# Down projection: h's high half times both halves of w2 in one product of 256 columns, the second sums evicted by ScalarE and added by GpSimd

## The chip, the cores and the metric

The kernel runs on one core of a Trainium2 chip (trn2). The metric is the device time of one execution in microseconds (us), median of several runs. The engines are PE (TensorE), DVE (VectorE), ACT (ScalarE), POOL (GpSimd) and SP (SyncE, which here only issues transfers).

## The reference

Attention with pooled keys comes first, and its rows go through a mixture of 8 experts, of which each row uses the one with the largest gate logit. The change lies wholly in the second part:

```python
def _moe_ref(x, w_skip, w_gate, w1, w2):          # x: 49152 rows of 128, F = 1024
    do_compute = x @ w_skip > 0
    xc = x[do_compute]
    logits = xc @ w_gate
    e_idx = np.argmax(logits, axis=1)
    ...                                           # gate_w: softmax weight of the chosen expert
    for e in range(8):
        mask = e_idx == e
        h = np.maximum(xc[mask] @ w1[e], 0.0)
        y[mask] = gate_w[mask, None] * (h @ w2[e])
    out = x.copy()
    out[do_compute] = xc + y
```

## The kernel before

The attention part writes its rows to a scratch buffer sorted by expert. The expert part takes them in **steps** of 512 rows (`ST`), four steps (`NST`) to a group of 2048 rows of one expert. There are 72 steps: 24 "peeled" ones (`peel`, written out, interleaved with the end of the attention), then a loop (`For_i`) whose body is one group, four stages s = 0 to 3, run for 12 iterations.

float32 numbers are split into two float16 halves, a high and a low one, so each product of the mathematics is three on PE: high·high, high·low, low·high. A step consists of:

- `up(s, cs)`: for each of 8 chunks of 128 hidden columns, three products of 512 columns into a PSUM tile `h_ps` (L296 to L298; in the peeled steps it is named `up_ps`; four buffers). ACT evicts relu as `h["hi"]` (L299), then DVE makes `h["lo"]` (L300) from the same PSUM tile, and only that frees the buffer.
- `x_transpose`: ACT (L282) and DVE (L285) split rows of a later step, and SP transposes them.
- `down(s)`: 24 terms (weight half, h half, chunk), four products of 128 columns each (one for each 128 rows), accumulated in four PSUM banks `ys[t]`, traced as `acc_ps` (L311). The halves of h are the loaded weights, `w2_hi` or `w2_lo` is streamed. `w2_lo` for chunk k comes two chunks after `w2_hi` (`WL = 2`).
- `finish(s)`, called in the next step: DVE computes `o = ys[t] * gate + x` (L323) for the four t, and POOL scatters the four blocks of rows to the output (L192).

Each engine executes its instructions in program order. In the loop's stage 0 a new expert's w2 has to be split: `split_w2()` stands between `up(s, range(1, 4))` and `gates(s)`, so on ACT w2's high half (L275) follows the fourth `h_hi`, and on DVE the low half (L276) follows the fourth `h_lo`. In stage 1 DVE finds the largest weights of the next expert (`w_scale`, L209 to L217) after its part of `x_transpose`, and the next step's `o` stands behind it. In stage 2 one small product (L220) belongs to the same work.

## Time and profile before

| | us |
|---|---|
| median of 3 runs | 1737.91 (1737.71 to 1739.04) |
| the profiled execution | 1737.34 |
| its span in the trace | 1735.6 |
| of it, PE busy / DVE / ACT / POOL | 1703.6 / 1525.8 / 1265.2 / 1024.7 |

The profiled execution is one run, 1.74 us longer than the span between its first and last instruction. Busy time of PE counts pipelined products until their modelled end, so it says that PE had work, not that it streamed at its peak. Starts in the timeline are exact to 0.01 us.

### The profile page before, as it was taken

How to read it: one execution, taken by the hardware profiler on the slowest of the kernel's cores; microseconds unless marked ns; L12 is line 12 of the kernel's file. 1: busy time of each engine (PE TensorE's matmuls, PEld its weight loads, DVE VectorE, ACT ScalarE, POOL GpSimd, SP SyncE). 2: the span in 40 equal slices, each digit the busy share in tenths (PEclk: the TensorE clock that was granted, in tenths of full speed). 3: DMA queues.
4: the chain of work that ended last, by engine and by line, in shares of the span. 5: the costliest groups of instructions: out<-in, count | busy, mean ns of one | idle time of the engine just before them, and what ended most of it. 6: DMA issues, size and time to landing. Idle time of an engine off the chain costs nothing.

```text
span 1735.6 us, 51351 instructions
## 1 busy us (share of the span) xinstructions
PE 1703.6 (98%) x18801; PEld 1426.6 (82%) x18801; DVE 1525.8 (88%) x3217; ACT 1265.2 (73%) x2399; POOL 1024.7 (59%) x1292
## 2 busy tenths in 40 slices
PE   6999999999999999999999999999999999999998
PEld 5999999999999989999999777777777777777776
DVE  7989999999999999999999877777888888888887
ACT  4888888888898888888888655555555556666664
POOL 3268878888788888765668445543333333343433
PEclk9999999999999999999999999999999999999999
DMA  8999999999899999999998666222433333333333
GB/s 239 220 242 204 198 199 228 228 200 184 175 194 206 226 218 202 183 199 198 203 202 186 175 193 149 89 83 75 93 102 103 99 97 99 100 107 101 97 99 86
DMA packets 616917, 281.18 MB, mean 162 GB/s; under 512 B 502944, under 2 KB 567072, under 8 KB 616736
## 3 DMA queue, kind: packets, MB, share of 16 engines
q1 hardware_dynamic: 590192, 231.68, 64.5%
q0 software_dynamic: 21504, 38.43, 7.0%
q10 hardware_dynamic: 5040, 8.72, 1.3%
q8 instruction: 106, 1.74, 0.5%
q14 instruction: 75, 0.61, 0.1%
HBM read 85.36 MB, written 79.72 MB: 95 GB/s over the span
## 4 chain that ended last, share of the span: by engine, by line
PE 82%; DVE 11%; DMA 2%; issue 2%; POOL 1%; ACT 1%; SPq 0%; POOLq 0%; DVEq 0%; ACTq 0%
PE acc_ps L311 22%; PE acc_ps L720 17%; PE s_ps L655 6%; PE s_ps L657 6%; PE s_ps L656 5%; PE h_ps L296 5%; PE h_ps L298 5%; PE h_ps L297 5%; DVE nm L663 4%; PE acc_ps L695 4%; PE up_ps L296 2%; PE up_ps L298 2%; PE up_ps L297 2%; DVE p L677 2%; DVE ptq L703 1%
## 5 line engine op out<-in xcount | busy, mean ns | idle before, releaser
L192 POOL DMA_INDIRECT scr<-rows,di x384 | 422.2, 1099 | 170.0 <-DVE nm L663 91.5
L669 ACT ACTIVATE p_sb<-s_ps,nm 128x768 f32<-128x768 f32 x384 | 346.8, 903 | 103.9 <-DVE nm L663 100.9
L192 POOL DMA_INDIRECT out_dram<-o,xin x196 | 201.6, 1029 | 318.5 <-DVE o L323 266.0
L663 DVE TENSOR_REDUCE nm<-s_ps 128x1 f32<-128x768 f32 x384 | 365.2, 951 | 19.0 <-PE s_ps L657 17.4
L299 ACT ACTIVATE h_hi<-h_ps 128x512 f16<-128x512 f32 x384 | 223.9, 598 | 206.9 <-PE h_ps L298 193.3
L720 PEld LDWEIGHTS <-pt 128*128 128x128 f16 x4608 | 274.8, 97 | 64.7 <-issue 63.0
L720 PE MATMUL acc_ps<-v_hi,pt 128*128 128x138 f16 x3072 | 320.1, 224 | 2.7 <-DVE rs L728 1.8
L311 PEld LDWEIGHTS <-h_hi 128*128 128x128 f16 x4608 | 287.6, 98 | 15.6
L655 PE MATMUL s_ps<-k_hi,q_hi 128*128 128x384 f32 x768 | 293.4, 382 | 0.4 <-ACT k_hi L520 0.4
L720 PE MATMUL acc_ps<-v_lo,pt 128*128 128x138 f16 x1536 | 293.0, 223 | 0.0
L677 DVE SCALAR_TENSOR_TENSOR p<-p_sb,p 128x512 f16<-128x512 f32 x384 | 276.9, 721 | 5.6 <-ACT p L673 4.8
L300 DVE SCALAR_TENSOR_TENSOR h_lo<-h_ps,h_hi 128x512 f16<-128x512 f32 x384 | 245.7, 687 | 19.4 <-ACT h_hi L299 17.9
L657 PE MATMUL s_ps<-k_hi,q_lo 128*128 128x384 f32 x768 | 259.4, 338 | 0.0
L656 PE MATMUL s_ps<-k_lo,q_hi 128*128 128x384 f32 x768 | 258.1, 336 | 1.0 <-DVE k_lo L521 1.0
L673 ACT ACTIVATE p<-p_sb 128x512 f16<-128x512 f32 x384 | 242.4, 631 | 12.5 <-DMA pt<-p 9.6
L311 PE MATMUL acc_ps<-w_hi,h_lo 128*128 128x128 f16 x2304 | 222.6, 219 | 0.0
L311 PE MATMUL acc_ps<-w_lo,h_hi 128*128 128x128 f16 x2304 | 210.9, 219 | 0.0
L311 PE MATMUL acc_ps<-w_hi,h_hi 128*128 128x128 f16 x2304 | 210.9, 219 | 0.0
L299 ACT ACTIVATE h_hi<-up_ps 128x512 f16<-128x512 f32 x192 | 114.5, 597 | 109.5 <-PE up_ps L298 100.9
L720 PE MATMUL acc_ps<-v_hi,ptq 128*128 128x138 f16 x1536 | 178.0, 223 | 0.0
L323 DVE SCALAR_TENSOR_TENSOR o<-acc_ps,g_sc,xin 128x128 f32<-128x128 f32 x288 | 81.0, 344 | 104.5 <-PE acc_ps L311 100.8
L720 PE MATMUL acc_ps<-v_lo,ptq 128*128 128x138 f16 x768 | 154.9, 223 | 0.0
(200 smaller groups left out, 3393.7 us busy)
## 6 DMA issues: line engine op xcount, KB each, us to landing
q_sb<-in_q_dram SPq DMA_DIRECT2D x96, 256.0 KB
out_dram<-rows SPq DMA_DIRECT2D x96, 256.0 KB
xin<-scr SPq DMA_DIRECT2D x75, 264.0 KB, 2.9
kvt<-in_kv_dram SPq DMA_DIRECT2D x74, 256.0 KB
w_raw<-in_moe_w_dram SPq DMA_DIRECT2D x26, 512.0 KB, 3.9
scr<-pad ACTq DMA_DIRECT2D x32, 264.0 KB
pt<-p SPq DMA_TRANSPOSE x384
scr<-rows,di POOLq DMA_INDIRECT x384
```

What stands on the lines that cost most here:

```text
L192: ins = nc.gpsimd.indirect_dma_start(out=dst, out_offset=bass.IndirectOffsetOnAxis(ap=ids, axis=0), in_=src, in_offset=None, bounds_check= ...
L299: nc.scalar.activation(out=h["hi"][:, c, :], in_=ps, func=AF.Relu)
L300: paced["by"] = nc.vector.scalar_tensor_tensor(out=h["lo"][:, c, :], in0=ps, scalar=0.0, in1=h["hi"][:, c, :], op0=ALU.max, op1=ALU.subtra ...
L311: m = nc.tensor.matmul(ys[t], h[x][:, k, t * P:(t + 1) * P], w[:, k, :], start=(i == 0), stop=(i == len(terms) - 1))
L655: nc.tensor.matmul(s[:, h, :HK], q_hi, k_hi[:, sl], start=True, stop=False)
L656: nc.tensor.matmul(s[:, h, :HK], q_hi, k_lo[:, sl], start=False, stop=False)
L657: nc.tensor.matmul(s[:, h, :HK], q_lo, k_hi[:, sl], start=False, stop=True)
L663: paced["by"] = nc.vector.tensor_reduce(out=NM[t], in_=S_PS[t][:, :, :HK], axis=AX.XY, op=ALU.max, negate=True).ins
L669: nc.scalar.activation(out=P_SB[t], in_=S_PS.pop(t)[:, :, :HK], func=AF.Exp, bias=NM.pop(t))
L673: nc.scalar.activation(out=P16[t][:, 0, :], in_=p_flat(t)[:, 0:KD * P], func=AF.Copy, scale=2.0 ** PEXP)
L677: paced["both"] = nc.vector.scalar_tensor_tensor(out=p16[:, 1, :], in0=p_flat(t)[:, 0:KD * P], scalar=2.0 ** PEXP, in1=p16[:, 0, :], op0=A ...
L720: nc.tensor.matmul(ps[:, j % 2, :], w, v[a][:, k, :], start=(i == 0), stop=(i == len(AVL) - 1))
```

## The change

The two halves of w2 lie side by side in one tile `w2_hl`, so that one product streams both of them (256 columns) past a loaded block of `h_hi`; `h_lo` still meets the high half alone. A step's `down` is then 16 terms of four products: 32 of 256 columns and 32 of 128. The second 128 columns of each bank hold the sums of `h_hi` with w2's low half. `finish` has DVE make `o` from the first half of the bank as before; ACT evicts the second half, times the gate, to a tile `o2` (t = 0, 1 at once; t = 2, 3 after the fourth `h_hi` of the next step); POOL adds `o2` to `o` and then scatters. After the last step DVE does both halves. The gates get two alternating places.

```diff
-    g_sc = wp.tile([P, 6 * TT], F32, name="g_sc")[:, 0:TT]
-    w2_hi = wp.tile([P, FC, C], F16, name="w2_hi")
-    w2_lo = wp.tile([P, FC, C], F16, name="w2_lo")
+    g_sc = wp.tile([P, 6 * TT], F32, name="g_sc")[:, 0:2 * TT]
+    w2_hl = wp.tile([P, FC, 2, C], F16, name="w2_hl")
+    w2_hi, w2_lo = w2_hl[:, :, 0, :], w2_hl[:, :, 1, :]
...
     def down(s):
         terms = []
-        for c in range(FC + WL):
-            for w, x, k in ((w2_hi, "hi", c), (w2_hi, "lo", c - DL), (w2_lo, "hi", c - WL)):
-                if 0 <= k < FC:
-                    terms.append((w, x, k))
-        for i, (w, x, k) in enumerate(terms):
+        for c in range(FC + DL):
+            terms.extend((x, k, n) for x, k, n in (("hi", c, 2), ("lo", c - DL, 1)) if 0 <= k < FC)
+        for i, (x, k, n) in enumerate(terms):
             for t in range(TT):
-                m = nc.tensor.matmul(ys[t], h[x][:, k, t * P:(t + 1) * P], w[:, k, :], start=(i == 0),
+                m = nc.tensor.matmul(ys[t][:, 0:n * C], h[x][:, k, t * P:(t + 1) * P],
+                                     w2_hl[:, k, 0:n, :].rearrange("p a c -> p (a c)"), start=(i == 0),
                                      stop=(i == len(terms) - 1))
...
-    def finish(s):
+    def finish(s, end=False):
         o = (first_p[0] if first_p else op).tile([P, TT, C], F32, name="o")
+        o2 = None if end else op.tile([P, TT, C], F32, name="o2", bufs=1)
+        ids = xin[s].bitcast(I32)
+
+        def second(ts):
+            for t in ts:
+                nc.scalar.activation(out=o2[:, t, :], in_=ys[t][:, C:2 * C], func=AF.Copy, scale=gate_of(s, t))
+
+        def send(ts):
+            for t in ts:
+                if not end:
+                    nc.gpsimd.tensor_tensor(out=o[:, t, :], in0=o[:, t, :], in1=o2[:, t, :], op=ALU.add)
+                if first_p:
+                    out_rows.append((out, kept[:, t:t + 1], o[:, t, :], NT - 1, "out"))
+                else:
+                    scatter_rows(out, ids[:, t, C + 1:C + 2], o[:, t, :], NT - 1, "out")
+
         for t in range(TT):
-            paced["by"] = nc.vector.scalar_tensor_tensor(out=o[:, t, :], in0=ys[t], scalar=g_sc[:, t:t + 1],
+            paced["by"] = nc.vector.scalar_tensor_tensor(out=o[:, t, :], in0=ys[t][:, 0:C], scalar=gate_of(s, t),
                                                          in1=xin[s][:, t, 0:C], op0=ALU.mult, op1=ALU.add).ins
-        ids = xin[s].bitcast(I32)
+            if end:
+                nc.vector.scalar_tensor_tensor(out=o[:, t, :], in0=ys[t][:, C:2 * C], scalar=gate_of(s, t),
+                                               in1=o[:, t, :], op0=ALU.mult, op1=ALU.add)
+        early, rest = range(TT // 2), range(TT // 2, TT)
+        if end:
+            send(range(TT))
+            return
+        second(early)
         if first_p:
             kept = first_p[0].tile([P, TT], I32, name="ids")
             nc.vector.tensor_copy(kept, ids[:, :, C + 1])
-            out_rows.extend((out, kept[:, t:t + 1], o[:, t, :], NT - 1, "out") for t in range(TT))
-            return
+        else:
+            yield
+        send(early)
         yield
-        for t in range(TT):
-            scatter_rows(out, ids[:, t, C + 1:C + 2], o[:, t, :], NT - 1, "out")
+        second(rest)
+        send(rest)
+        yield
...
-                    next(done, None)
+                    next(done)
                     up(s, range(1, 4))
                     for eng in (nc.vector, nc.scalar):
                         tc.previous_stage_wait(eng.engine)
+                    next(done)
                     if s == 0:
                         split_w2()
                     gates(s)
...
-        for _ in finish(NST - 1):
+        for _ in finish(NST - 1, True):
```

Three places show how the instructions then stand. On PE, at the start of the down projection in the loop's stage 0, these rows stood before (the end of `up`, the first block of `h_hi`, and, 38 rows left out, the first use of w2's low half; in brackets are the semaphores waited for, those ending in stg0 counted by instructions of this stage 0):

```order
L297 LDWEIGHTS w_hi
L297 MATMUL h_ps<-xT_145,w_hi 128x512
L298 LDWEIGHTS w_lo
L298 MATMUL h_ps<-xT_145,w_lo 128x512
L311 LDWEIGHTS h_hi [waits PE_49,Activation_I-23941_stg0]
L311 MATMUL acc_ps<-w_hi,h_hi 128x128 [waits Activation_I-23941_stg0]
...
L311 LDWEIGHTS h_hi
L311 MATMUL acc_ps<-w_lo,h_hi 128x128 [waits DVE_I-23941_stg0]
```

At the same place these stand now (the last two are the first block of `h_lo`):

```order
L297 LDWEIGHTS w_hi
L297 MATMUL h_ps<-xT_144,w_hi 128x512
L298 LDWEIGHTS w_lo
L298 MATMUL h_ps<-xT_144,w_lo 128x512
L309 LDWEIGHTS h_hi [waits PE_49,Activation_I-23379_stg0,Pool_49]
L309 MATMUL acc_ps<-w_hl,h_hi 128x256 [waits DVE_I-23379_stg0]
...
L309 LDWEIGHTS h_lo
L309 MATMUL acc_ps<-w_hl,h_lo 128x128
```

The wait for DVE's low half of w2 moved from the twenty-first product of the down projection to its first.

On ACT, the rows of stage 0 were these before:

```order
L299 ACTIVATE h_hi<-h_ps 128x512 [waits sem_stage_2_38996,PE_I-23941_stg0,DVE_49,PE_49,Activation_49,Pool_49]
L299 ACTIVATE h_hi<-h_ps 128x512 [waits PE_I-23941_stg0] x3
L275 ACTIVATE w_hi<-w_raw,w_sc 128x1024 [waits Activation_49,DVE_49,PE_49]
L299 ACTIVATE h_hi<-h_ps 128x512 [waits PE_I-23941_stg0] x4
L282 ACTIVATE x_144<-xin_142 128x128 [waits DMASW5_49,DMASW6_49,DMASW4_49,DMASW7_49,DMAHW7_49,DMAHW0_49,DMAHW6_49,DMAHW1_49,DVE_49,Activation_49]
```

And now (L330 is `second`; its output `o2` is printed as `o` with a number):

```order
L330 ACTIVATE o_23390<-acc_ps,g_sc 128x128 [waits sem_stage_2_37476,DVE_49,DVE_I-23379_stg0,PE_49,Activation_49,Pool_49]
L330 ACTIVATE o_23390<-acc_ps,g_sc 128x128 [waits PE_49,DVE_I-23379_stg0]
L299 ACTIVATE h_hi<-h_ps 128x512 [waits PE_I-23379_stg0,DVE_49,Activation_49]
L299 ACTIVATE h_hi<-h_ps 128x512 [waits PE_I-23379_stg0] x3
L330 ACTIVATE o_23390<-acc_ps,g_sc 128x128 [waits Activation_49,PE_49,DVE_I-23379_stg0]
L330 ACTIVATE o_23390<-acc_ps,g_sc 128x128 [waits PE_49,DVE_I-23379_stg0]
L275 ACTIVATE w_hl<-w_raw,w_sc 128x8x128 [waits DVE_49,Activation_49,PE_49]
L299 ACTIVATE h_hi<-h_ps 128x512 [waits PE_I-23379_stg0] x4
L282 ACTIVATE x_143<-xin_141 128x128 [waits DMASW5_49,DMASW6_49,DMASW4_49,DMASW7_49,DMAHW7_49,DMAHW0_49,DMAHW6_49,DMAHW1_49,DVE_49,Activation_49]
```

Two evictions came ahead of the first `h_hi`, and two between the fourth `h_hi` and w2's high half.

On ACT in stage 2, these rows stood before:

```order
L299 ACTIVATE h_hi<-h_ps 128x512 [waits sem_stage_0_38994,PE_I-23941_stg2,DVE_I-23941_stg1,PE_I-23941_stg1]
L299 ACTIVATE h_hi<-h_ps 128x512 [waits PE_I-23941_stg2,DVE_I-23941_stg1,PE_I-23941_stg1] x3
L299 ACTIVATE h_hi<-h_ps 128x512 [waits Activation_I-23941_stg1,PE_I-23941_stg2,DVE_I-23941_stg1,PE_I-23941_stg1]
L299 ACTIVATE h_hi<-h_ps 128x512 [waits PE_I-23941_stg2,DVE_I-23941_stg1,PE_I-23941_stg1] x3
L282 ACTIVATE x_144<-xin_140 128x128 [waits DMAHW1_I-23941_stg1,DMAHW0_I-23941_stg1,DVE_I-23941_stg1]
```

And now:

```order
L330 ACTIVATE o_23742<-acc_ps,g_sc 128x128 [waits sem_stage_0_37474,DVE_I-23379_stg2,DVE_I-23379_stg1,Pool_I-23379_stg1]
L330 ACTIVATE o_23742<-acc_ps,g_sc 128x128 [waits DVE_I-23379_stg2]
L299 ACTIVATE h_hi<-h_ps 128x512 [waits PE_I-23379_stg2] x4
L330 ACTIVATE o_23742<-acc_ps,g_sc 128x128 [waits Activation_I-23379_stg1,DVE_I-23379_stg2]
L330 ACTIVATE o_23742<-acc_ps,g_sc 128x128 [waits DVE_I-23379_stg2]
L299 ACTIVATE h_hi<-h_ps 128x512 [waits PE_I-23379_stg2,DVE_I-23379_stg1] x4
L282 ACTIVATE x_143<-xin_139 128x128 [waits DMAHW1_I-23379_stg1,DMAHW0_I-23379_stg1,DVE_I-23379_stg1]
```

Two evictions stand ahead of the step's first `h_hi`, and each waits for an instruction of DVE in the same stage (DVE_..._stg2), the `o` (L342 there, L323 before) that reads the same bank.

## Rows read from the trace of the kernel before

**Rows 1.** The page: the chain that ended last, shares of the span by line.

```profile
PE acc_ps L311 22%; PE acc_ps L720 17%; PE s_ps L655 6%; PE s_ps L657 6%; PE s_ps L656 5%; PE h_ps L296 5%; PE h_ps L298 5%; PE h_ps L297 5%; DVE nm L663 4%; PE acc_ps L695 4%; PE up_ps L296 2%; PE up_ps L298 2%; PE up_ps L297 2%; DVE p L677 2%; DVE ptq L703 1%
```

**Rows 2.** Windows, the loop: length, then PE, PEld, DVE, ACT, POOL busy.

```profile
1225.00:1727.00 502.00, 501.83 (x5718) 367.02 (x5716) 423.68 (x972) 297.47 (x589) 193.91 (x189) 1.00 0.37 100
```

**Rows 3.** Source view: products of w2's low half, splits of w2 (ns min/median/max).

```profile
L311 PE MATMUL acc_ps<-w_lo,h_hi x2304: 219/219/219, 968.7 to 1727.0; 128*128 128x128 f16 x192
...
L276 DVE SCALAR_TENSOR_TENSOR w_lo<-w_raw,w_sc,w_hi x13: 1280/1284/1285, 958.4 to 1689.2; 128x1024 f16<-128x1024 f32 x13
```

**Rows 4.** Timeline of PE, one stage 0: start, length of the merged row.

```profile
1387.74 0.38 PE L296 MATMUL h_ps<-xT,w_hi 128*128 128x512 f16 x1
...
1392.92 0.61 PE L311 MATMUL acc_ps<-w_hi,h_hi 128*128 128x128 f16 x8
...
1394.03 0.39 PE L311 MATMUL acc_ps<-w_lo,h_hi 128*128 128x128 f16 x4
...
1398.28 0.38 PE L296 MATMUL h_ps<-xT,w_hi 128*128 128x512 f16 x1
```

**Rows 5.** Timeline of PE, stage 2: the one product of 256 columns.

```profile
1414.00 0.27 PE L220 MATMUL h_ps<-w_dg,ones_bf 128*128 128x256 bf16 x1
1414.11 0.61 PE L311 MATMUL acc_ps<-w_hi,h_hi 128*128 128x128 f16 x8
```

**Rows 6.** Timeline of ACT, the same stage 0.

```profile
1388.75 2.37 ACT L299 ACTIVATE h_hi<-h_ps 128x512 f16<-128x512 f32 x4 [3.44 <-PE h_ps L298]
1391.02 1.14 ACT L275 ACTIVATE w_hi<-w_raw,w_sc 128x1024 f16<-128x1024 f32 x1
1392.06 2.05 ACT L299 ACTIVATE h_hi<-h_ps 128x512 f16<-128x512 f32 x4
```

**Rows 7.** Timeline of DVE, the same stage 0.

```profile
1387.62 1.12 DVE L323 SCALAR_TENSOR_TENSOR o<-acc_ps,g_sc,xin 128x128 f32<-128x128 f32 x4 [1.00 <-PE acc_ps L311]
...
1392.19 1.28 DVE L276 SCALAR_TENSOR_TENSOR w_lo<-w_raw,w_sc,w_hi 128x1024 f16<-128x1024 f32 x1 [0.33 <-ACT w_hi L275]
```

**Rows 8.** Groups by line: busy us, mean ns of one.

```profile
L735 ACT ACTIVATE rows<-acc_ps,rs 128x138 f32<-128x138 f32 x384 | 120.8, 367 | 0.0
L299 ACT ACTIVATE h_hi<-h_ps 128x512 f16<-128x512 f32 x384 | 223.9, 598 | 206.9 <-PE h_ps L298 193.3
L300 DVE SCALAR_TENSOR_TENSOR h_lo<-h_ps,h_hi 128x512 f16<-128x512 f32 x384 | 245.7, 687 | 19.4 <-ACT h_hi L299 17.9
L323 DVE SCALAR_TENSOR_TENSOR o<-acc_ps,g_sc,xin 128x128 f32<-128x128 f32 x288 | 81.0, 344 | 104.5 <-PE acc_ps L311 100.8
```

**Rows 9.** Timeline of ACT: two evictions from PSUM in a row.

```profile
966.99 0.64 ACT L735 ACTIVATE rows<-acc_ps,rs 128x138 f32<-128x138 f32 x2
```

**Rows 10.** Timeline of ACT, stages 1 and 2.

```profile
1399.21 5.12 ACT L299 ACTIVATE h_hi<-h_ps 128x512 f16<-128x512 f32 x8 [3.94 <-PE h_ps L298]
...
1409.75 5.12 ACT L299 ACTIVATE h_hi<-h_ps 128x512 f16<-128x512 f32 x8 [4.25 <-PE h_ps L298]
```

**Rows 11.** Timeline of DVE, stage 1 and the start of stage 2.

```profile
1402.52 2.54 DVE L300 SCALAR_TENSOR_TENSOR h_lo<-h_ps,h_hi 128x512 f16<-128x512 f32 x4
...
1409.13 1.12 DVE L323 SCALAR_TENSOR_TENSOR o<-acc_ps,g_sc,xin 128x128 f32<-128x128 f32 x4
1410.38 2.63 DVE L300 SCALAR_TENSOR_TENSOR h_lo<-h_ps,h_hi 128x512 f16<-128x512 f32 x4
```

**Rows 12.** Timeline of PE, stage 2: first products of chunks 0 and 4.

```profile
1408.82 0.38 PE L296 MATMUL h_ps<-xT,w_hi 128*128 128x512 f16 x1
...
1411.41 0.38 PE L296 MATMUL h_ps<-xT,w_hi 128*128 128x512 f16 x1
```

**Rows 13.** Timeline of DVE and POOL after the last step.

```profile
1727.17 1.12 DVE L323 SCALAR_TENSOR_TENSOR o<-acc_ps,g_sc,xin 128x128 f32<-128x128 f32 x4 [1.08 <-PE acc_ps L311]
1727.87 0.98 POOL L192 DMA_INDIRECT out_dram<-o,xin  x1 [5.33 <-DVE o L323]
```

**Rows 14.** Groups by line: an add of POOL on 128 by 128.

```profile
L492 POOL TENSOR_TENSOR pooled<-kvt 128x128 f32<-128x128 f32 x19 | 9.3, 488 | 3.8 <-DVE mx L771 1.9 <-DVE p L677 1.5
```

More of the change, by code (lines that the diff above doesn't have):

```diff
@@ L52 @@
     XC = 4
-    DL, WL = 1, 2
+    DL = 1
     XP = 3
@@ L312, in down, with gate_of @@
                                      stop=(i == len(terms) - 1))
-            if i % 6 == 5:
+            if i % 4 == 3:
                 paced["by"] = m.ins
                 yield
+    def gate_of(s, t=0, n=1):
+        return g_sc[:, s % 2 * TT + t:s % 2 * TT + t + n]
     def gates(s):
-        nc.vector.tensor_scalar(out=g_sc, in0=xin[s][:, :, C], scalar1=y_sc[:, 0:1], scalar2=None, op0=ALU.mult)
-    def finish(s):
+        nc.vector.tensor_scalar(out=gate_of(s, 0, TT), in0=xin[s][:, :, C], scalar1=y_sc[:, 0:1], scalar2=None,
+                                op0=ALU.mult)
@@ L394, in peel @@
             s, last = b % NST, b == LB - 1
+            done = finish((b - 1) % NST) if b > 0 else iter(())
             if b > 0:
-                for _ in finish((b - 1) % NST):
-                    pass
+                next(done)
                 if b + 3 < LB:
@@ L405, in peel @@
                 if c == XP:
+                    next(done, None)
                     gates(s)
@@ L415, in peel @@
             if b == 0:
-                ys.extend(acc_ps()[:, 0:C] for _ in range(TT))
+                ys.extend(acc_ps()[:, 0:2 * C] for _ in range(TT))
             for d, _ in enumerate(down(s)):
@@ L1088 @@
                         tc.previous_stage_wait(eng.engine)
+                    next(done)
                     if s == 0:
```

## The prediction

> **What bounds the kernel now.** First the chain that ended last [rows 1]: the change touches the down projection (`acc_ps L311`, 22% of the span), and around it stand the products of `up` (`h_ps`, `up_ps`), all of them PE. Then the windows over the loop [rows 2]: in 502.00 us PE is busy 501.83 at granted clock 1.00, DVE 423.68, ACT 297.47, POOL 193.91. So the expert part is as long as PE's stream, and the question is twofold: how much shorter the stream gets, and whether one of the others, which now have slack, comes to hold PE up. For the second I read the timelines of one iteration engine by engine; the reader is to see in them how close ACT and DVE run to the moment at which PE needs their result.
>
> **What is saved on PE.** Columns do not change: a step streams 96 x 128 before, 32 x 256 + 32 x 128 now, 12288 both times. What goes are 32 weight loads and 32 starts of a product. In stage 0 [rows 4] 24 products of 512 columns run from 1387.74 to 1392.92, 5.18 us or 215.8 ns each, and 96 of 128 columns from 1392.92 to 1398.28, 5.36 us or 55.8 ns each. The line through both gives 160.0/384 = 0.417 ns a column and 2.5 ns a product, so 109.2 ns for 256 columns. The only such product in the trace takes 1414.11 - 1414.00 = 0.11 us to the next start [rows 5], which fits. Two of 128 cost 111.7 ns, so a pair saves 2.5 ns; there are 2304 pairs (the count of w2-low products, [rows 3]): **-5.8 us**. Bounds: nothing if 256 columns cost twice 128, and 2304 x 5.0 = 11.5 us if the wide product had no fixed part at all.
>
> **What is late in stage 0.** This is the largest term. The split of a new w2 runs while `up` runs: ACT's four `h_hi` from 1388.75, the high half 1391.02 to 1392.16 [rows 6], DVE's low half 1392.19 to 1393.47 [rows 7], 0.03 us behind ACT. PE starts the down projection at 1392.92 but meets w2's low half only at 1394.03 [rows 4]: 0.56 us to spare. Now its first product streams the low half too; in the instruction order the wait for it stands at that product. Alone this makes PE wait until 1393.47 + 0.03 = 1393.50, 0.58 us. And ACT has two evictions of the last step's sums ahead of the split. The nearest row is an eviction of 138 PSUM columns: 0.37 us each [rows 8], but two in a row take 0.64 [rows 9], so each further one costs 0.27; at the same rate the split comes 0.55 late. DVE waits for it, so the low half ends at 1394.02 and PE waits until 1394.05: 1.13 us. The loop has 12 iterations (13 splits, the first before the loop, [rows 3]): **+13.6 us**. Bounds: 12 x 0.58 = 7.0 if the evictions cost ACT nothing, 12 x 1.31 = 15.8 if they don't overlap (2 x 0.367 in place of 0.55). I take 0.27, since the row is the same kind of instruction on nearly the same width. PE has no slack later in which to win this back [rows 2].
>
> **What is late in stage 2.** Two evictions also stand ahead of a step's first `h_hi`, each behind DVE's `o` for the same bank. Where `o` starts as soon as PE ends, that is hidden: ACT idles 3.9 us before `h_hi` [rows 10], and the second eviction is through within 0.05 us of the moment at which the first chunk is ready. But `o` of stage 2 is late already: DVE finds the largest weights at the end of stage 1, and `o` starts at 1409.13, 0.31 us after PE began the step at 1408.82 [rows 11, 12]. Step by step:
> In stage 1 `h_hi` come every (5.12 - 0.60)/7 = 0.65 us from 1399.21 [rows 8, 10], PE's pace; ACT alone needs (2.05 - 0.60)/3 = 0.48 [rows 6]. With 0.55 of evictions between, the fifth starts at 1399.21 + 3 x 0.65 + 0.48 + 0.55 = 1402.19, not 1401.81, ends at 1402.79, and DVE's fifth `h_lo` starts at 1402.82, not 1402.52 [rows 11]: 0.30 late. Its four `h_lo` win back some 0.05; the rest of DVE's stage has no idle time, so `o` is 0.25 late, and another 0.09 against PE, whose step is shorter by 32 x 2.5 ns: 0.65 us after PE's start. Four `o` take 1.12, so they start (1.12 - 0.34)/3 = 0.26 apart; the second ends 0.26 + 0.34 later at 1.25 [rows 8, 11], the second eviction starts at 1.28, `h_hi` 0.27 behind it at 1.55, and 0.60 + 0.03 later DVE's first `h_lo` at 2.18, ending at 2.87 [rows 8]. PE needs that buffer for chunk 4 at 1411.41 - 1408.82 = 2.59 [rows 12]. Before, `h_lo` ended at 1410.38 + 0.69 = 1411.07, 0.34 to spare; now PE waits 0.31 us, 12 times: **+3.7 us**. Bounds: 0, if 0.3 of the many small terms is too much; with evictions that don't overlap 0.37 more (0.19 in stage 1, 0.10 before `h_hi`, the rest rounded up), 12 x 0.68 = 8.2.
>
> The Trainium skill ("PSUM — Partial Sum Buffer", section "PSUM bank collisions raise a hardware error") says that two engines must not touch one PSUM bank at the same time, two readers included, and that software has to order them. This is a rule against the change, since a bank that DVE alone read is now read by two engines in turn. By it the 3.7 us stand; if ACT could evict while DVE reads, `h_hi` would not be late, the first `h_lo` would wait for `o` alone, and the sum would be 3.7 us smaller. The instruction order has the wait; no row of before shows the two engines on one bank.
>
> **The rest.** POOL gets four adds a step, but for the last step, at 0.49 us for the same shape [rows 14], 2.0 us in a step of 10.5 (half the way from 1387.74 to 1408.82, [rows 4, 12]). It is busy 194 of 502 us [rows 2], so its own idle time hides them; were that cover gone, the scatters would be late, and with them the loads into the rows' buffers on SP's queue and the transposes behind those. In the peeled steps w2 is not split; the largest weights are found once, so the stall of stage 2 comes once more: +0.3. After the last step the first scatter starts 1727.87 - 1727.17 - 0.34 = 0.36 us behind the first `o` [rows 8, 13]; now each `o` takes two instructions, and in program order the second of the first block comes two starts later: 2 x 0.26 = +0.5 us.
>
> **The sum** for the profiled execution: 1737.34 - 5.8 + 13.6 + 3.7 + 0.3 + 0.5 = 1749.6. The median of the runs stands 0.57 above that execution: **1750.2 us**, +0.7%. The forecast is slower.
>
> **Rivals.**
> A, only stage 0 pays. The chain of stage 2 sums small terms against a slack of 0.34, and each 0.1 less on ACT or DVE cuts it by as much. Against: `o` is late there already. Then the time is 1750.2 - 4.0 = 1746.2.
> B, not slower: the fixed part of every product shrinks as loads thin out, so that the down projection runs at bare columns, 12288 x 0.417 = 5.12 us in place of 5.36 a step, 72 x 0.24 = -17.3 in place of -5.8. That gives 1738.7, no change. For it: no row shows a stream with so few loads among products of these widths. Against: products of 512 columns, with loads that have much time, show the same 2.5 ns. It decides from 2304 pairs x 7.9 ns, the 18.1 us that the waits cost.
> C, POOL's adds hold DVE up: an add of 0.49 us [rows 14] just ahead of w2's low half in stage 0 makes that later by as much, 12 x 0.49 = 5.9, and one ahead of DVE's row work in stage 1 passes on to stage 2, 5.9 more: 1762. For it: the first eviction of stage 0 ends near 1388.3; two adds and two scatters of 0.98 [rows 13] with some 0.3 ahead of each bring the third add to about 1391.9 to 1392.4, near the split at 1392.74. Against: it ends before. The Trainium skill ("SBUF — State Buffer", section "Who interferes with whom") has DVE and GpSimd share a pair of ports to SBUF under an exclusive lock, which would be the cause; no run here shows it with these two instructions.
>
> **Chances.** Forecast 0.62, A 0.23, C 0.10, B 0.05. The likeliest time is 1750.2. The range reaches down to A less 2 us (evictions cheaper than 0.27), 1744, and up to evictions that don't overlap (+2.2 in stage 0, +4.5 in stage 2), 1757; that leaves out B and C, under 2 in 10 with what A and the forecast may miss. A measurement of this kernel tells some 0.2% (3.5 us) from no change. Faster by more than that takes B with a free eviction as well: 0.02; within it, B: 0.03; slower: 0.95.
>
> **What would show it.** In the trace after: in each stage 0 a gap of about 1.1 us on PE between the last product of `up` and the first of L309, released by DVE's low half; in stage 2 about 0.3 us before chunk 4, released by `h_lo`; down projections of stages 1 and 3 some 0.08 us shorter than 5.36; w2's high half about 0.55 later behind the fourth `h_hi`. The prediction is wrong if PE starts stage 0's down projection without a gap (then ACT's split did not slip and the wait is not where the order puts it), if a down projection shortens by more than 0.2 us, or if PE waits in other stages, for rows or for POOL.

## The result and the profile after

The changed kernel takes 1756.77 us, median of 5 runs (1755.35 to 1757.51), beside 1737.91 for the kernel before: a ratio of 1.0106, 95% interval 1.0091 to 1.0121. It is slower by 18.9 us. The forecast was 1750.2 and the range ended at 1757.0, so the sign was right, the size was some 6.6 us short, and the range held by 0.2 us. The profiled execution took 1756.8, its span 1754.2.

Four moments cut each span into parts that can be compared: the first product of the down projection, the first of `h_ps` (the loop's first step), the last down product, the end. They are the first and last starts in the tile views of `acc_ps` and `h_ps`.

| us | first down | steps ahead of the loop | loop | end |
|---|---|---|---|---|
| before | 967.6 | 250.4 | 509.0 | 8.6 |
| after | 967.2 | 253.0 | 522.9 | 11.1 |

The loop has 13.9 of the 18.6 us, the steps ahead of it 2.6, the end 2.5. The waits of PE, longest sums first (engine, tile and line, releaser; total, times, longest; the lines left out between are of the attention part):

```profile
PE acc_ps L309 <- DVE w_hl L276: 11.2, 11, 1.3
...
PE h_ps L296 <- DVE h_lo L300: 3.6, 12, 0.3
PE up_ps L296 <- DVE h_lo L300: 3.3, 4, 2.6
```

The first two are the forecast's two stalls. The twelfth wait of stage 0 stands further down, 1.0 us put down to `y_sc`, DVE's short copy behind the split. Of the third row, ahead of the loop, one wait of 2.6 us was not forecast. These rows count from the modelled end of the product before, so they show 0.16 us less a time than the gaps below, which count from the moment at which the next product could have started. The windows view of the loop, columns as in [rows 2], shows the other side: PE is busy 500.47 of 515.00 us, where before it was busy in all but 0.17 of 502.00.

```profile
1228.00:1743.00 515.00, 500.47 (x4198) 345.75 (x4196) 425.83 (x972) 328.87 (x776) 288.05 (x379) 1.00 0.36 96
```

One stage 0 on PE (it answers to [rows 4]):

```profile
1389.65 1.04 PE L309 MATMUL acc_ps<-w_hl,h_hi 128*128 128x256 f16 x8
...
1394.93 0.38 PE L296 MATMUL h_ps<-xT,w_hi 128*128 128x512 f16 x1
...
1399.90 0.38 PE L298 MATMUL h_ps<-xT,w_lo 128*128 128x512 f16 x1
1401.25 0.92 PE L309 MATMUL acc_ps<-w_hl,h_hi 128*128 128x256 f16 x7 [0.97 <-DVE y_sc L278]
```

A down step without a stall takes 1394.93 - 1389.65 = 5.28 us, 0.08 less than before. In stage 0 the next product after the one at 1399.90 could start 0.216 later, at 1400.12; it starts 1.13 later than that. ACT, DVE and POOL in the same stage [rows 6, 7]:

```profile
1396.01 2.31 ACT L299 ACTIVATE h_hi<-h_ps 128x512 f16<-128x512 f32 x4
1398.22 0.62 ACT L330 ACTIVATE o<-acc_ps,g_sc 128x128 f32<-128x128 f32 x2
1398.72 1.16 ACT L275 ACTIVATE w_hl<-w_raw,w_sc 128x1024 f16<-128x1024 f32 x1
```

```profile
1399.91 1.28 DVE L276 SCALAR_TENSOR_TENSOR w_hl<-w_raw,w_sc,w_hl 128x1024 f16<-128x1024 f32 x1 [0.79 <-ACT w_hl L275]
```

```profile
1399.96 1.54 POOL L335 TENSOR_TENSOR o<-o,o 128x128 f32<-128x128 f32 x1
```

ACT's two evictions take 0.50 us ahead of the split, DVE waits for the high half (0.79 us idle), and PE for DVE. GpSimd's third add starts 0.05 us behind the split and takes 1.54 us, where the median is 0.47; the split keeps its 1.28. So it is in ten of the twelve iterations. In the second (split at 1268.99, add at 1269.04) the add keeps 0.47 and the split takes 1.61, in the first the split takes 1.52; there the gap is 1.45 and 1.37. Stage 2, DVE, then ACT, then PE [rows 10 to 12]:

```profile
1417.67 1.12 DVE L342 SCALAR_TENSOR_TENSOR o<-acc_ps,g_sc,xin 128x128 f32<-128x128 f32 x4
1419.29 1.89 DVE L300 SCALAR_TENSOR_TENSOR h_lo<-h_ps,h_hi 128x512 f16<-128x512 f32 x3 [0.49 <-ACT h_hi L299]
```

```profile
1418.14 0.62 ACT L330 ACTIVATE o<-acc_ps,g_sc 128x128 f32<-128x128 f32 x2 [4.42 <-DVE o L342]
1418.66 2.06 ACT L299 ACTIVATE h_hi<-h_ps 128x512 f16<-128x512 f32 x4
```

```profile
1416.98 0.38 PE L296 MATMUL h_ps<-xT,w_hi 128*128 128x512 f16 x1
...
1419.36 0.38 PE L298 MATMUL h_ps<-xT,w_lo 128*128 128x512 f16 x1
1420.03 0.38 PE L296 MATMUL h_ps<-xT,w_hi 128*128 128x512 f16 x1 [0.30 <-DVE h_lo L300]
```

`o` starts 0.69 after the step, the second sums follow, the first `h_hi` behind them, DVE idles 0.49 for it, and PE's fifth chunk starts 1420.03 - 1419.36 - 0.22 = 0.45 us late. The long stall ahead of the loop, on DVE, then on PE by windows (length, PE busy, granted clock, DMA share, GB/s):

```profile
1039.37 1.13 DVE L342 SCALAR_TENSOR_TENSOR o<-acc_ps,g_sc,xin 128x128 f32<-128x128 f32 x4 [5.55 <-DMA out_dram<-o,ids]
```

```profile
1036.00:1038.00 2.00, 2.00 (x17) 1.00 1.18 253
1038.00:1040.00 2.00, 1.08 (x6) 1.00 0.41 96
1040.00:1042.00 2.00, 0.29 (x2) 1.00 0.50 176
1042.00:1044.00 2.00, 2.00 (x8) 0.61 1.00 316
1044.00:1046.00 2.00, 2.00 (x7) 0.54 0.39 152
```

A new `o` waits 5.55 us until the scatter out of its buffer has landed; PE runs dry for 2.8 us and goes on at 1041.71; from 1042.43 to 1045.84, 3.4 us, its granted clock is 0.50, the lower level of 1.2 GHz (0.61 and 0.54 over the two windows). At the end, SP (its last load, then its waits over the loop, longest first) and DVE:

```profile
1742.62 0.35 SPq L198 DMA_DIRECT2D xin<-scr  x1
```

```profile
SPq L198 <- DMA out_dram<-o,xin: 208.9, 111, 3.8
```

```profile
1745.38 0.61 DVE L342 SCALAR_TENSOR_TENSOR o<-acc_ps,g_sc,xin 128x128 f32<-128x128 f32 x2 [3.08 <-PEq L1105]
```

PE's last product starts at 1743.1, yet DVE's first eviction comes 2.3 us later; before it came 0.2 us later [rows 13]. The profile puts its wait down to the branch that ends the loop (L1105); SP's loads of rows (L198) wait for scatters to land, and e6 tests whether that brings SP there late.

### The profile page after: what moved, and what is told of

Its sections match the earlier page's. It is cut to its first block, busy times and chain, and to the rows that moved or that the text cites. A ratio compares the mean times of both kernels' runs of the same rounds, so it can differ in the third digit from the quotient of the medians.

```text
span 1754.2 us, 47456 instructions
## 1 busy us (share of the span) xinstructions
PE 1700.2 (97%) x16497; PEld 1393.2 (79%) x16497; DVE 1532.2 (87%) x3221; ACT 1311.9 (75%) x2683; POOL 1156.6 (66%) x1576
## 3 DMA queue, kind: packets, MB, share of 16 engines
q8 instruction: 98, 1.61, 0.4%
## 5 line engine op out<-in xcount | busy, mean ns | idle before, releaser
L309 PE MATMUL acc_ps<-w_hl,h_hi 128*128 128x256 f16 x2304 | 333.9, 273 | 12.2 <-DVE w_hl L276 11.2
L330 ACT ACTIVATE o<-acc_ps,g_sc 128x128 f32<-128x128 f32 x284 | 89.1, 369 | 271.8 <-DVE o L342 271.8
L335 POOL TENSOR_TENSOR o<-o,o 128x128 f32<-128x128 f32 x284 | 141.3, 506 | 200.0 <-ACT o L330 191.8
L300 DVE SCALAR_TENSOR_TENSOR h_lo<-h_ps,h_hi 128x512 f16<-128x512 f32 x384 | 238.3, 683 | 28.1 <-ACT h_hi L299 27.6
L192 POOL DMA_INDIRECT out_dram<-o,xin x196 | 195.7, 998 | 83.8 <-POOL o L335 70.5
L309 PEld LDWEIGHTS <-h_hi 128*128 128x128 f16 x2304 | 207.3, 98 | 43.3 <-issue 16.0
L299 ACT ACTIVATE h_hi<-h_ps 128x512 f16<-128x512 f32 x384 | 212.4, 606 | 5.3 <-PE h_ps L298 0.2
L309 PE MATMUL acc_ps<-w_hl,h_lo 128*128 128x128 f16 x2304 | 210.9, 219 | 0.0
L309 PEld LDWEIGHTS <-h_lo 128*128 128x128 f16 x2304 | 170.9, 98 | 11.5
L342 DVE SCALAR_TENSOR_TENSOR o<-acc_ps,g_sc,xin 128x128 f32<-128x128 f32 x288 | 81.2, 344 | 103.6 <-PE acc_ps L309 57.5
```

Source lines behind the costliest of these rows:

```text
L192: ins = nc.gpsimd.indirect_dma_start(out=dst, out_offset=bass.IndirectOffsetOnAxis(ap=ids, axis=0), in_=src, in_offset=None, bounds_check= ...
L299: nc.scalar.activation(out=h["hi"][:, c, :], in_=ps, func=AF.Relu)
L300: paced["by"] = nc.vector.scalar_tensor_tensor(out=h["lo"][:, c, :], in0=ps, scalar=0.0, in1=h["hi"][:, c, :], op0=ALU.max, op1=ALU.subtra ...
L309: m = nc.tensor.matmul(ys[t][:, 0:n * C], h[x][:, k, t * P:(t + 1) * P], w2_hl[:, k, 0:n, :].rearrange("p a c -> p (a c)"), start=(i == 0) ...
```

## The experiments

Runs stand in the order in which they were made, four to a chip. On the second and third chip the kernel before takes 15 to 17 us more than on the first (no profile of it exists there). So ratios are taken against the kernel before on the same chip, and of the parts only loop and end are compared across chips.

| run | us, median | before beside it | ratio (95%) | ahead of loop | loop | end |
|---|---|---|---|---|---|---|
| e1_narrow | 1765.9 | 1737.62 | 1.0161 (1.0144 to 1.0177) | 257.8 | 528.2 | 11.0 |
| b1_low_at_once | 1725.11 | 1737.62 | 0.993 (0.9915 to 0.9945) | 244.3 | 503.0 | 8.6 |
| e2_split_first | 1751.2 | 1737.62 | 1.0075 (1.006 to 1.0089) | 253.5 | 516.2 | 11.2 |
| e3_pieces | 1742.82 | 1737.62 | 1.0029 (1.0017 to 1.004) | 251.1 | 509.5 | 11.1 |
| e4_second_late | 1773.98 | 1754.82 | 1.0101 (1.0075 to 1.0127) | 259.9 | 527.5 | 12.0 |
| e5_hold | 1764.65 | 1754.82 | 1.0055 (1.0034 to 1.0076) | 257.5 | 523.5 | 11.0 |
| e6_ids | 1765.67 | 1754.82 | 1.0058 (1.0039 to 1.0078) | 258.8 | 520.4 | 8.9 |
| e7_no_add | 1755.06 | 1754.82 | 1.0003 (0.9991 to 1.0015) | 252.7 | 520.5 | 9.0 |
| r_after | 1766.31 | 1752.99 | 1.0072 (1.0059 to 1.0085) | 258.4 | 524.1 | 11.1 |
| e8_scale_late | 1768.06 | 1752.99 | 1.0082 (1.0069 to 1.0095) | 258.4 | 526.5 | 11.1 |
| e9_all_mended | 1749.49 | 1752.99 | 0.9982 (0.9971 to 0.9992) | 253.8 | 512.8 | 8.9 |
| b2_low_first | 1759.17 | 1752.99 | 1.0039 (1.0026 to 1.0052) | 262.5 | 516.1 | 8.6 |

**What the width saves.**

```diff
-                m = nc.tensor.matmul(ys[t][:, 0:n * C], h[x][:, k, t * P:(t + 1) * P],
-                                     w2_hl[:, k, 0:n, :].rearrange("p a c -> p (a c)"), start=(i == 0),
-                                     stop=(i == len(terms) - 1))
+                for a in range(n):
+                    m = nc.tensor.matmul(ys[t][:, a * C:(a + 1) * C], h[x][:, k, t * P:(t + 1) * P],
+                                         w2_hl[:, k, a, :], start=(i == 0 and a == 0),
+                                         stop=(i == len(terms) - 1))
```

> The changed kernel, with each product of 256 columns made as two of 128 (h's high half stays the weights of both). If the width alone saves 2.5 ns a pair, 2304 pairs give back 5.8 us: 1762.5 us, with a down step of 5.36 us again, and stage 0's wait for w2's low half still 1.1 us a time. The short gaps of 0.15 us on PE at the loop's edge, which went away with the change and which nobody forecast, are a second question: if they hang on how many instructions PE has to be fed, they come back (1.8 us more, 1764.3); if on something else in the change, they stay away. Rival: two products of 128 with the same weights cost what one of 256 does, so 1756.8 and a step of 5.28.

1765.9 us where 1762.5 or 1764.3 was expected. Each half product also loads its block of h anew (18801 weight loads in the run, 16497 in the changed kernel), so the edit puts back loads and starts alike. The down step is 5.36 us again. The loop grew by 5.3 us: 48 steps x 0.08 = 3.8, 2.1 at the loop's edge and 0.4 more in stage 0, less 1.0 in stage 2, whose gap is 0.38 in place of 0.45 since PE's longer step takes 0.08 from it. The edge on PE, this run first, the changed kernel second:

```profile
1446.02 0.61 PE L310 MATMUL acc_ps<-w_hl,h_lo 128*128 128x128 f16 x8
1446.67 0.38 PE L296 MATMUL h_ps<-xT,w_hi 128*128 128x512 f16 x1
```

```profile
1438.02 0.61 PE L309 MATMUL acc_ps<-w_hl,h_lo 128*128 128x128 f16 x8
1438.47 0.38 PE L296 MATMUL h_ps<-xT,w_hi 128*128 128x512 f16 x1
```

Eight products of 55.8 ns are 0.45 us; the next step starts 0.65 behind them with narrow products, 0.45 with wide ones. So the short gap at the edge hangs on how many products, or how narrow ones, PE has there; which of the two is not shown. The other 4.8 us stand ahead of the loop: 24 x 0.08 = 1.9, a stall near 1041 us that is longer here (3.8 instead of 2.8 us), and 6.8 us at the lower clock behind it in place of 3.4.

**The early need alone, first try.**

```diff
-    DL, WL = 1, 2
+    DL, WL = 1, 0
```

> The kernel before, with w2's low half multiplied in the same place as its high half instead of two chunks later; nothing of the evictions is changed. Theory of the sum: PE now needs w2's low half at the start of the down step, 0.55 to 0.58 us before DVE has it, so 12 waits of 0.55: 1744.5 to 1745 us. Rival: stage 0's wait comes from what the change added on ScalarE and GpSimd, and the early need alone costs nothing that can be measured: 1737.9 us.

It came out faster, and for a reason that has nothing to do with the question: with this number the list of products ends one chunk early, and the last chunk's product with `h_lo` is left out (2016 in place of 2304).

```profile
L311 PE MATMUL acc_ps<-w_hi,h_lo x2016: 219/219/219, 967.0 to 1713.4; 128*128 128x128 f16 x184
```

288 x 55.8 ns are 16.1 us; with them the time would be 1741.2. Of use is only the gap in stage 0: 0.39 us, four products (0.22) into the step, so the low half comes 0.61 behind the step's start.

**ScalarE's share of stage 0.**

```diff
-                    next(done)
                     if s == 0:
                         split_w2()
+                    next(done)
```

> The changed kernel, with w2's split in stage 0 put ahead of ScalarE's last two second evictions instead of behind them. Theory of the sum: the split starts 0.55 us earlier, the wait in stage 0 goes from 1.13 to 0.55 or 0.6, 12 times: 1750 us. Rival: the wait comes from GpSimd's adds beside DVE's low half, and the order on ScalarE does not matter: 1756.8 us, wait of 1.1 as before.

The loop fell by 6.7 us; the gap is 0.61 us in every stage 0, half of what it was:

```profile
PE acc_ps L309 <- DVE w_hl L276: 5.0, 11, 0.5
```

Both halves of the term are shown: 0.52 us a time from the evictions, 0.61 from the need for the low half at the start.

**The low half in pieces.**

```diff
-    def split_w2():
+    def split_w2(n=1):
+        for i in range(n):
+            sl = slice(i * FC // n, (i + 1) * FC // n)
+            nc.scalar.activation(out=w2_hi[:, sl, :], in_=w2_raw[:, sl, :], func=AF.Copy, scale=w_sc[:, 1:2])
...
-                        split_w2()
+                        split_w2(4)
```

> The changed kernel, with stage 0's split of w2 made in four pieces of two chunks, high and low in turn. Theory: PE waits because the whole low half has to be there before the first product; the first piece is there about 0.4 us after ScalarE's last second eviction plus 0.4 on DVE, before PE is through with the up step, so stage 0's wait goes: 14.1 us less, 1742.7 us, less up to 2 us for the overheads of six more instructions in each stage 0. Rival: ScalarE and DVE are themselves behind by then, the later pieces come late and PE waits for each in turn: 1750 us or more.

1742.82 us against 1742.7 expected: the gap in stage 0 is gone and the loop is 13.4 us shorter. What remains for PE in the expert part is the other two stalls:

```profile
PE h_ps L298 <- DVE h_lo L302: 4.2, 12, 0.4
PE up_ps L298 <- DVE h_lo L302: 3.0, 4, 2.4
```

**Stage 2, ScalarE's part moved.** `finish` got a flag with which the first two second evictions, their adds and scatters stand behind the fourth chunk.

```diff
-                    done = finish(prv)
+                    done = finish(prv, late=s == 2)
```

> The changed kernel, with ScalarE's first two second evictions in stage 2 of the loop (and GpSimd's adds and scatters behind them) put behind the up step's fourth chunk instead of ahead of its first. Theory of the sum: they are what makes h's first high and low halves late there, so PE's wait ahead of the fifth chunk, 0.45 us x 12, goes: 5.4 us less, 1751.4 us. Rival: DVE itself is late in stage 2 (its new rows of o start 0.69 us after the step), and moving ScalarE's part gives nothing: 1756.8, the wait still there, released by h's low half.

The fifth chunk no longer waits, but the product that finds w's scale does, at the end of the up step, 0.58 us x 12:

```profile
1296.34 1.13 ACT L330 ACTIVATE o<-acc_ps,g_sc 128x128 f32<-128x128 f32 x4
1297.34 2.08 ACT L299 ACTIVATE h_hi<-h_ps 128x512 f16<-128x512 f32 x4
```

```profile
1298.74 0.28 PE L220 MATMUL h_ps<-w_dg,ones_bf 128*128 128x256 bf16 x1 [0.42 <-DVE h_lo L300]
```

Four evictions in a row now hold the fifth `h_hi`, and the buffer that the scale's product needs comes free as late. Neither theory had this place. The loop is 4.6 us longer: 1.6 here, and 2.9 in stage 0, where the gap is 1.45 in 10 of 12 iterations.

**The order of the scatters.**

```diff
-        if scr_rows and len(out_rows) <= (HOLD - 1) * TT:
+        if scr_rows and len(out_rows) <= (HOLD - 1) * TT - TT // 2:
```

> The changed kernel, with two numbers' worth of room put back in the order of the scatters in the steps ahead of the loop: a row of o goes out ahead of a row of the scratch table from 19 held rows on, not from 21, since the change hands over rows of o two and two. Theory: the one stall of 2.8 us at 1041 us and the slow clock behind it (1.4 us) come from an o that waits for a scatter two rows late, so both go: 4 us less, 1752.8 us, the steps ahead of the loop 249 instead of 253 us. Rival: the DMA queues are full there in any order and the transfers land late anyway: 1756.8, with the stall.

The stall at 1041 us is gone (e4 and e6 have it on the same chip, with 4.0 and 3.0 us), and so is the fall of the clock there; `o` now waits for PE only:

```profile
1039.85 1.13 DVE L342 SCALAR_TENSOR_TENSOR o<-acc_ps,g_sc,xin 128x128 f32<-128x128 f32 x4 [2.54 <-PE acc_ps L309]
```

The total does not show 4 us: the steps ahead of the loop take 257.5 us, where e4 and e6 have 259.9 and 258.8. Other stalls come later on this chip: about 0.64 us in each of six steps between 1075 and 1156 us, 1.1 at 1064 and 2.3 at 1132.69, with 3.4 us at the lower clock behind that. The 0.6 stand in e4, e6 and (with 0.5) in r_after, e8 and e9 as well.

**The row numbers copied.**

```diff
         else:
             yield
+            kept = op.tile([P, TT], I32, name="ids")
+            nc.gpsimd.tensor_copy(kept, ids[:, :, C + 1])
...
-                    scatter_rows(out, ids[:, t, C + 1:C + 2], o[:, t, :], NT - 1, "out")
+                    scatter_rows(out, ids[:, t, C + 1:C + 2] if end else kept[:, t:t + 1], o[:, t, :], NT - 1,
+                                 "out")
```

> The changed kernel, with the row numbers of a step in the loop copied by GpSimd into a tile of their own ahead of its adds, so that SyncE's next load of rows no longer waits for the last scatter. Theory: behind the loop DVE's first eviction waits for the barrier that SyncE reaches late, because its last load waits for GpSimd's last scatters; with the copy that end is 2.1 us earlier: 1754.7 us, 9 instead of 11.1 us from PE's last product to the end. Rival: GpSimd itself reaches the barrier as late: 1756.8. Either way nothing changes in the loop, since the loads have a step of slack.

The end is 8.9 instead of 11.1 us, as expected: DVE's first eviction follows PE at once.

```profile
1753.37 0.61 DVE L343 SCALAR_TENSOR_TENSOR o<-acc_ps,g_sc,xin 128x128 f32<-128x128 f32 x2 [0.94 <-PE acc_ps L309]
```

But "nothing changes in the loop" was wrong: the loop became 2.5 us shorter. Between GpSimd's first add and first scatter of a step lie 0.28 us of idle time here and 0.78 in the changed kernel, so its last add starts 6.22 us after PE's step instead of 6.71. In stage 1 of the changed kernel the last add runs beside DVE's four low halves of x, which take 1.31 us; here it ends before them, and they take 1.13. The changed kernel first, POOL, then DVE; then this run:

```profile
1413.23 0.47 POOL L335 TENSOR_TENSOR o<-o,o 128x128 f32<-128x128 f32 x1
```

```profile
1413.35 1.31 DVE L285 SCALAR_TENSOR_TENSOR x<-xin,x 128x128 f16<-128x128 f32 x4
```

```profile
1424.23 0.46 POOL L335 TENSOR_TENSOR o<-o,o 128x128 f32<-128x128 f32 x1
```

```profile
1424.84 1.13 DVE L285 SCALAR_TENSOR_TENSOR x<-xin,x 128x128 f16<-128x128 f32 x4
```

With 0.18 us less there, stage 2's gap is 0.28 us instead of 0.45, 12 times, and stage 0's is 1.13 or 1.15 in all twelve iterations. That GpSimd and DVE hold each other up is what the Trainium skill has in "SBUF — State Buffer", section "Who interferes with whom"; these rows agree, with 0.18 us on DVE here.

**Without the adds.** The line with GpSimd's `tensor_tensor` is left out.

> The changed kernel without GpSimd's adds (the second sums are evicted by ScalarE and then dropped, so the part of w2's low half is left out of the rows in all blocks but the last). Theory of the sum: the adds cost DVE next to nothing, so only what hangs on GpSimd's time goes: up to 2.1 us behind the loop and 0.6 us in the first two stage 0; the stall at 1041 us stays, since it is made by the order of the scatters: 1754 us. Rival C of the forecast: the adds hold DVE up in every step, and without them 8 to 10 us go, 1748 us, with shorter durations of DVE's low halves.

The loop is 520.5 us, as with the copy, with the same 0.28 in stage 2 and 1.15 in stage 0: in the loop the adds cost 2.4 us, not the 8 to 10 of rival C. The stall near 1041 us shrank to 0.9 us (4.0 and 3.0 in e4 and e6 on the same chip), so it is not the order of the scatters alone: GpSimd's time counts there too. The ratio fell more than loop and end explain. The rest lies ahead of the loop: the six stalls of 0.6 us, which e4, e5 and e6 have on this chip, are not there, and `o` follows PE at once. Why the adds' absence does that stays open.

**The changed kernel again**, unaltered.

> The changed kernel once more, beside the three below on one chip, since the last four runs had a chip on which the kernel before took 17 us more: a ratio to before of 1.0106, within 0.002, and the stall near 1041 us again. If the stall hangs on how fast that chip's transfers land, its length may differ from 2.8 us, between 1 and 4 us.

The ratio is lower than expected, 1.0072. The loop is as it was (524.1 us, 1.2 more, since the gap in stage 0 is 1.45 in five of twelve iterations). In these five DVE's split takes 1.60 to 1.61 us in place of 1.28. DVE in one of them, then POOL:

```profile
1276.31 1.61 DVE L276 SCALAR_TENSOR_TENSOR w_hl<-w_raw,w_sc,w_hl 128x1024 f16<-128x1024 f32 x1 [0.79 <-ACT w_hl L275]
```

```profile
1276.36 0.47 POOL L335 TENSOR_TENSOR o<-o,o 128x128 f32<-128x128 f32 x1
1277.11 1.68 POOL L192 DMA_INDIRECT out_dram<-o,xin  x1 [0.28 <-POOL o L335]
```

The scatter beside it takes 1.68 us, but that is not what holds the split: the kernel before has such a scatter beside a split of 1.28 [rows 7], and e6 has eleven of 1.68 beside splits of 1.28 to 1.30.

```profile
1392.62 1.71 POOL L192 DMA_INDIRECT out_dram<-o,xin  x1 [0.30 <-issue]
```

What goes with the longer split is the add 0.05 us behind it. In each of these five iterations it keeps its 0.47; in the six with a gap of 1.13 it starts as close behind, takes 1.54, and the split keeps its 1.28. One of the two pays.

Stall and slow clock near 1044 us are there again, the stall 3.6 us long.

**Stage 2, DVE's part moved.** A `yield` in `w_scale` parts its maxima from the four short operations behind them.

```diff
                     next(done)
+                    if s == 2:
+                        next(scale)
                     up(s, range(1, 4))
-                        scale = w_scale()
+                        scale = w_scale(late=True)
```

> The changed kernel, with DVE's four short operations on w's scale in stage 2 (0.73 us) put behind its rows of o and the first low half instead of ahead of the rows. Theory: the rows of o start 0.1 instead of 0.69 us after the step, as in stages 1 and 3, which have no wait, so the 0.45 us x 12 on PE in stage 2 go: 5.4 us less than the changed kernel beside it, 1751.4 us. Rival: DVE has no room for them anywhere in the up step, and the wait moves to a later chunk or to the product of the scale, as when ScalarE's part was moved: 1756.8 or more.

The rival held. `o` starts 0.04 us after the step, but the wait moves from the fifth chunk to the sixth and grows to 0.60 us:

```profile
1294.39 1.12 DVE L344 SCALAR_TENSOR_TENSOR o<-acc_ps,g_sc,xin 128x128 f32<-128x128 f32 x4
1295.98 0.69 DVE L302 SCALAR_TENSOR_TENSOR h_lo<-h_ps,h_hi 128x512 f16<-128x512 f32 x1 [0.47 <-ACT h_hi L301]
...
1296.98 0.59 DVE L219 TENSOR_SCALAR w_dg<-ident_bf,w_exp 128x128 bf16<-128x128 bf16 x2
1297.46 1.87 DVE L302 SCALAR_TENSOR_TENSOR h_lo<-h_ps,h_hi 128x512 f16<-128x512 f32 x3
```

DVE still idles 0.47 us for the first `h_hi`, which stands behind ScalarE's two evictions; in stages 1 and 3 PE's four buffers cover that idle time, in stage 2 they do not cover it and the short operations as well, in either of the two places tried.

**All four mended** (the edits of e3, e5, e6 and e8 together).

> The changed kernel with four edits together: w2's split in four pieces, the short operations on the scale behind the rows of o, the room in the order of the scatters, the row numbers copied. By the ledger: loop 522.9 - 13.4 - 5.4 = 504, steps ahead of the loop 249 to 251, end 9: 1732 us, some 6 us faster than before (ratio 0.9966), which is what the wider product gives PE and no more. Rival: a mended wait turns into the next one (GpSimd's adds beside DVE, PE's chunk behind the pieces), 1736 us or more, no faster than before.

16.8 us less than the changed kernel on the same chip, and 0.18% faster than before, 0.08 to 0.29% by the interval; half of what the ledger had. Stage 0 has no gap, the end is 8.9 us, the stall near 1041 us is gone. Stage 2 took most of the rest: a gap of 0.79 us x 12, where e8 alone has 0.60 and e3 alone 0.48 to 0.61. That the edit of e8 is what does harm here is not shown:

```profile
PE h_ps L300 <- DVE h_lo L304: 7.6, 12, 0.6
```

The edits of e3, e5 and e6 without that of e8 were not run.

**The early need alone, with all products.**

```diff
-        for c in range(FC + WL):
-            for w, x, k in ((w2_hi, "hi", c), (w2_hi, "lo", c - DL), (w2_lo, "hi", c - WL)):
+        for c in range(FC + DL):
+            for w, x, k in ((w2_lo, "hi", c), (w2_hi, "hi", c), (w2_hi, "lo", c - DL)):
```

> The kernel before, with all its products, and w2's low half multiplied ahead of its high half in each chunk, so that the down step begins with it. Theory: stage 0 then waits for the low half for 0.55 us (0.39 where four products ran ahead of it), 12 times, and nothing else changes: 1737.9 + 6.6 = 1744.5 us, ratio 1.0038. Rival: the early need makes other waits too (the last h_lo closer behind), 1748 us or more; or hides the wait in stage 0 elsewhere, 1738.

A ratio of 1.0039 where 1.0038 was expected. PE waits 0.61 us in each of the twelve stages 0, 7.3 us in all, and goes on 0.06 us behind the end of DVE's split. The loop is 7.1 us longer than before.

## Why the prediction was right, and by how much it was off

The direction and the two stalls of the loop came as forecast; the range held by luck. Its upper end stood for evictions that do not overlap, and these overlapped (0.50 us for two); what filled it came ahead of the loop and at its end. By its own terms, in us of the profiled executions:

| term | forecast | measured |
|---|---|---|
| PE, 2304 pairs | -5.8 | 72 x 0.08 = -5.8 |
| stage 0 | +13.6 | 1.37 + 1.45 + 10 x 1.13 = +14.1 |
| stage 2 | +3.7 | 12 x 0.45 = +5.4 |
| steps ahead of the loop | +0.3 | +4.5 |
| end | +0.5 | +2.5 |
| PE at the loop's edge (what the loop's +13.9 leaves) | 0 | -1.8 |
| attention part, and outside the span | 0 | -0.4, +0.9 |
| sum | +12.3 | +19.4 |

**PE** was right, by the down step of 5.28 us and by e1. Rival B, bare columns, fell with it.

**Stage 0** was right to 0.03 us in the two parts of which it was made: 0.58 forecast for the early need (0.61 in e2 and b2), 0.55 for the evictions (0.50 on ACT, 0.52 by e2). That their sum came out at 1.13 to the hundredth is luck, since the two errors cancel. Two iterations, more on other chips, have 0.2 to 0.3 us on top, where DVE's split and not GpSimd's add pays for their meeting. The prediction's reason against rival C, that the third add ends before the split, did not hold: it starts 0.05 us behind it.

**Stage 2** had the right mechanism and a size 0.14 us short; rival A is out. The chain left out what GpSimd does to DVE in stage 1: without an add beside the low halves of x (e6, e7) the gap is 0.28. That this is close to the 0.31 of the sum is luck in part: `o` then starts 0.52 us behind PE's step, where the chain had 0.65, and from `o` to the first `h_lo` it is 1.61, where the chain had 1.53. So 0.17 x 12 = 2.0 us of rival C happen at the second of its two places, DVE's row work in stage 1, for 0.18 us of an add and not 0.49; at the first, w2's split, 0.6 us in all. The prediction said that no row of before shows the two engines on one bank; `h_hi` and `h_lo` there read one `h_ps` tile in turn [rows 8]. That ScalarE's evictions are a cause is shown by the idle time of DVE behind them and by e4, where the fifth chunk starts without a wait; neither move (e4, e8) took the stall away, it came back in another place of the same up step.

**Ahead of the loop** is the step that failed: "the stall of stage 2 comes once more: +0.3". It comes (0.25, 0.40 and 0.22 near 1202 us), but the cost is a stall that no term had, 2.8 us and about 1.7 more at the lower clock (half of 3.4). It is one of the prediction's own signs of being wrong: PE waits, by way of `o`, for a scatter of POOL. "Its own idle time hides them" was said of GpSimd's adds, and the prediction named what would be late if that cover were gone, the scatters. They were late, for two reasons: the rows of `o` are handed over two and two, so a scratch row goes ahead of them (e5 takes the stall away), and the adds take GpSimd's time (e7 leaves 0.9 us of it). That the whole cost goes with the stall is not shown, since e5 ran on a chip with other stalls.

**The end** was mis-sized: 0.5 us for DVE's second instruction was nearly right (e6 and e7 end in 8.9 and 9.0, 0.3 to 0.4 above before), but 2.1 more come from SP, whose last load of rows waits for GpSimd's last scatter, which reads the row numbers out of the same tile. The copy of e6 shows it.

Open are the 0.9 us outside the span, and what makes the steps ahead of the loop longer on those two chips. Why the change costs less there can be added up for the third chip, if the kernel before behaves there as b2 does. Ahead of the loop b2 has 262.5 us, 12.1 more than the kernel before in its trace above; r_after has 258.4, 5.4 more than the changed kernel in its. The difference is 6.7 us, less 1.2 by which r_after's loop is longer 5.5; the change costs 13.3 us in place of 18.9. Two rows belong to it, PE in b2 and DVE in r_after:

```profile
PE acc_ps L311 <- issue: 12.5, 22, 1.1
```

```profile
1076.09 1.13 DVE L342 SCALAR_TENSOR_TENSOR o<-acc_ps,g_sc,xin 128x128 f32<-128x128 f32 x4 [3.34 <-issue]
```

Both wait for nothing that the profile names. Of the 22 times on PE, 15 (9.3 us, up to 1.1 each) stand between 1045 and 1153 us, in steps that are written out and not looped; the other seven are waits of stage 0 in the loop, which hang on DVE's split. In r_after `o` starts 0.79 us behind PE's step, where the trace of the changed kernel above has 0.09, and the stalls of 0.5 us follow.

## What to carry to other kernels

When two products become one, the merged one waits for the later of its two inputs: look for the step in which that input is fresh, and hand it over in pieces (here 13.4 of 18.9 us). A helper on an engine with slack is paid in every step where another engine waits behind it, and in what reads the same tile at the end of its queue: cost its place in each queue, not its busy time. Where a step is full on two engines, moving a short operation moves the stall; count the room of the whole step first.

## What the runs showed of the hardware

- After PE had stood almost still for 2.8 us (busy 1.08 and 0.29 in two windows of 2 us), it ran 0.7 us at full clock, then 3.4 us at a granted clock of 0.50, with products of 512 columns 0.43 us apart in place of 0.216. In e3 a stall of 2.5 us at the same place (busy 0.81 and 0.83 in such windows) had no fall behind it; in e5 one of 2.3 us at 1132.69 had, and in r_after one of 3.6.
- Where GpSimd's add started some 0.05 us behind DVE's split of w2, one of the two paid, and a few ns decided which. In after, r_after, e4 and e8 the starts in the traces lie 42 to 48 ns apart where the split took 1.60 to 1.61 us in place of 1.28 and the add kept its 0.47; they lie 48 to 53 ns apart where the add took 1.54 and the split kept its 1.28.
- A scatter that began during the split took 1.68 to 1.78 us in place of 0.99, before the change too, and the split kept its 1.28 to 1.30. Beside an add, four low halves of x took 1.31 in place of 1.13.
- At the edge of the loop PE lost 0.15 to 0.22 us an iteration with 96 narrow products in the step, and nothing with 64 that stream as many columns.
